# Gate sums in small steps, and the last row of each chunk one block ahead, in a fused recurrence and feed-forward kernel

## The chip, the cores and the metric

The kernel runs on one core of one Trainium2 chip. The metric is the device time of one execution in microseconds (us); of several executions the median counts. A core has TensorE (PE in the rows; the loading of its weights is PEld), VectorE (DVE), ScalarE (ACT), GpSimd (POOL), and SyncE (SP), which here issues every DMA. Each engine works through its own list of instructions in the order in which the program was built.

## What is computed

First a gated recurrence (mLSTM) over 768 steps for 4 batches with 8 heads of dimension 40, then a two-layer feed-forward network (320 to 2048 to 320) over the 3072 resulting rows:

```python
for t in range(S):
    m_new = np.maximum(f_gate[:, :, t] + m, i_gate[:, :, t])
    f_stab = np.exp(f_gate[:, :, t] + m - m_new)
    i_stab = np.exp(i_gate[:, :, t] - m_new)
    m = m_new
    C = f_stab[...] * C + i_stab[...] * np.einsum('bhd,bhe->bhde', vt, kt)
    n = f_stab[...] * n + i_stab[...] * kt
    h_tilde = np.einsum('bhde,bhe->bhd', C, qt)
    denom = np.maximum(np.abs(np.einsum('bhd,bhd->bh', n, qt)), 1.0)
    y[:, :, t] = sigmoid(o_gate[:, :, t]) * h_tilde / denom
h = y @ w_in
g = where(h >= 1, h, where(h <= -1, 0, (h + 1)**2 / 4))
out = g @ w_out
```

(The gates are abridged with "..." for added axes, and the sigmoid is written by name.)

## The kernel before

The 768 steps are cut into 6 chunks of 128, so that there are 24 pieces (chunk, batch), called rows here and numbered n = 4 * chunk + batch. The recurrence is done by chunk: inside a chunk it is a masked product of scores, and between chunks a state `C` is carried. The feed-forward network works on tiles of 512 tokens; tile j is chunk j of all four batches, so that rows 4j to 4j+3 make tile j, and tile j can begin only when its last row, 4j+3, is in `xh` and `xl` (y transposed and split in two words).

**The blocks.** Tile j has 16 blocks. Block x = 16 j + fc is `mm1` (8 products of 512 columns into a bank `psh`), the activation (`r`, on ACT twice and DVE once), the split of `r` into `gh` and `gl` (ACT, DVE), and two blocks later `mm2` (12 products of 320 columns into `pso`; 4 in tile 0). The loop over x at the end of the kernel sets the order in which all is written; a scheduler may then change the order within each engine's list.

**A row.** In the block that `OFFS` gives, a row of the next tile goes through `prep` (POOL masks the decay sums `Abc`, ACT takes 8 exponentials of them, POOL scales v), `score` (scores on PE, multiplied into `Abc` by DVE: the decayed scores), and `main` (PE: `psa<-C,qn` and then decayed scores times v; DVE: `hv`, `z`, `y`; PE: transposes `psa<-ident,y`; ACT: `CAST xh`; DVE: `xl`). `prep` stands 4 blocks ahead of `score`, `main` 3 blocks behind it, in three steps.

**Split scores.** From row 8 on, the decayed scores and v are cut into three bf16 parts (`parts3`: two instructions on DVE, `m<-Abc` and `v<-v`, and two on POOL for each row), and every head is multiplied in 6 part products: 48 products of 41 columns for a row. Rows 0 to 7 use the fp32 words: 8 products, which the trace shows as 16.

**Buffers.** `Abc` has three buffers. The DMA for row n+3 (`load_A`, from DRAM tensor `a_d`) is written in the first step of `main` of row n, and it waits until PE has read the scores of row n. It is issued by SP, like all others, in order.

**Gates.** For each chunk a piece of 16 small DVE instructions on 32 partitions (three of them scans), 3 on ACT, one on POOL, a transpose (`psa<-ident,ex`), the exponentials `G`, and 5 small DMAs (`a_d`, `dc_d`, three `dec`) gives the decays. Chunk j+2 is done in one go in block 3 of tile j, that is at x = 3, 19, 35 and 51.

Of the kernel before, what the change touches and what calls it, by code (L numbers as in the profile page):

```python
# [17 lines left out]
B, H, S, D = 4, 8, 768, 40  # L18
# [20 lines left out]

FRONT = 22  # L40
EARLY = 8
OFFS = [3, 5, 7, 9, 14, 18, 22, 25, 30, 34, 37, 40, 46, 48, 52, 56, 60, 66, 70, 74]
LEAD = 4
MLAG = 3
NA = 3
ST = 0

GFC = 3
DUE = lambda fc: 3 + fc


# [10 lines left out]
SPLIT_FROM = 8  # L62
# [33 lines left out]
def mlstm_ffn_kernel(ctx, tc, qk, qn, vk, og, fi0, fi, w_in, w_out, cst, out):  # L96
# [16 lines left out]
    later = ctx.enter_context(tc.tile_pool(name="later", bufs=1))  # L113
# [64 lines left out]
    exs = {}  # L178
    gtail = {}

    def gate_piece(c):
        gate_sums(c)
        gate_tail(c)
        gate_exps(c)

    def gate_sums(c):
        pool, i, f = gsrc.pop(c)

        NP = NSEQ if c else 3 * NSEQ
        new = lambda name, p=NP, n=L, bufs=1: pool.tile([p, n], F32, name=name if c else name + "0", bufs=bufs)  # L190
        k = 1
        m, a, ah, ac = new("m", n=L + 1, bufs=k), f, new("ah", bufs=k), new("ac")
        al = ah

        ex = exs[c] = new("ex", P)
        if c:
            nc.vector.tensor_copy(m[:, 0:1], carry)
        else:
            nc.vector.memset(m[:, 0:1], -1e30)
        nc.vector.tensor_tensor_scan(out=m[:, 1:], data0=f, data1=i, initial=m[:, 0:1], op0=ALU.add, op1=ALU.max)  # L200
        nc.vector.tensor_tensor(out=a, in0=f, in1=m[:, :L], op=ALU.add)
        nc.vector.tensor_tensor(out=a, in0=a, in1=m[:, 1:], op=ALU.subtract)

        nc.vector.tensor_scalar(out=ah, in0=a, scalar1=CLAMP, scalar2=GRID, op0=ALU.max, op1=ALU.add)
        nc.vector.tensor_scalar(out=ah, in0=ah, scalar1=-GRID, scalar2=None, op0=ALU.add)
        nc.vector.tensor_tensor_scan(out=ac, data0=rst[:NP], data1=ah, initial=0.0, op0=ALU.mult, op1=ALU.add)
        if c > 0:
            nc.sync.dma_start(a_d[c], ac)
            nc.scalar.copy(ex[64:96], ac)
        else:  # L210

            for p in (2 * NSEQ, NSEQ):
                nc.vector.tensor_tensor(out=ac[:p], in0=ac[:p], in1=top(ac[:p]), op=ALU.subtract)
            T["ac"] = ac
            m, a, ah, ac, al, i = (x[2 * NSEQ:] for x in (m, a, ah, ac, al, i))
            nc.gpsimd.tensor_copy(ex[64:96], ac)
        nc.vector.scalar_tensor_tensor(out=a, in0=a, scalar=CLAMP, in1=ah, op0=ALU.max, op1=ALU.subtract)
        reset = rst[:NSEQ] if c else rst[2 * NSEQ:]
        nc.vector.tensor_tensor_scan(out=al, data0=reset, data1=a, initial=0.0, op0=ALU.mult, op1=ALU.add)
        if c:  # L220
            nc.scalar.mul(ex[96:128], al, -1.0)
        else:
            nc.gpsimd.tensor_scalar(out=ex[96:128], in0=al, scalar1=-1.0, scalar2=None, op0=ALU.mult)
        nc.vector.tensor_copy(carry, m[:, L:])
        gtail[c] = i, m, a, ac, al, ex

    def gate_tail(c):
        i, m, a, ac, al, ex = gtail.pop(c)
        dh = m[:, :L]
        eng = nc.vector  # L230
        eng.tensor_tensor(out=a, in0=i, in1=m[:, 1:], op=ALU.subtract)
        eng.tensor_tensor(out=a, in0=a, in1=al, op=ALU.subtract)
        nc.gpsimd.tensor_copy(ex[0:32], a)
        eng.tensor_tensor(out=dh, in0=ac[:, L - 1:].broadcast_to([NSEQ, L]), in1=ac, op=ALU.subtract)
        eng.tensor_tensor(out=dh, in0=dh, in1=a, op=ALU.add)
        eng.tensor_tensor(out=ex[32:64], in0=dh, in1=al[:, L - 1:].broadcast_to([NSEQ, L]), op=ALU.add)
        eng.tensor_tensor(out=dc[:, c:c + 1], in0=ac[:, L - 1:], in1=al[:, L - 1:], op=ALU.add)

# [316 lines left out]
    def main(n):  # L555

        c, b = divmod(n, B)
        t = T.pop(n) if n >= B else T[n]
        g = gates_of(n)
        sg = sig[c][:, b, :]  # L560
        M = t["A"]
        if c > 0:
            C = state[b]
            ip = psum_a()
            for gi, h0 in enumerate(GROUPS):
                o = 6 - h0 if gi == 2 else 0
                nc.tensor.matmul(ip[:, (h0 + o) * D1:(h0 + 3) * D1], t["qn"][:, gi, :], C[:, gi, o * D1:3 * D1],
                                 start=True, stop=True)
            hv = wk.tile([P, H, D1], F32, name="hv", bufs=2)
            iv = ip[:, :H * D1].rearrange("p (h d) -> p h d", d=D1)  # L570
            nc.vector.tensor_tensor(out=hv, in0=iv, in1=g[:, 2, :].unsqueeze(2).broadcast_to([P, H, D1]), op=ALU.mult)
        up = psum_a()
        hot(up)
        if n < SPLIT_FROM:
            for h in range(H):
                nc.tensor.matmul(up[:, h * D1:(h + 1) * D1], M[:, h, :], t["v1"][:, h, :], start=True, stop=True)
        else:
            prod = [(i, k) for i in range(3) for k in range(3 - i)]
# [12 lines left out]
        if n >= B:
            load_A(n + NA)
        yield

        z = wk.tile([P, H], F32, name="z")
        nc.vector.scalar_tensor_tensor(out=z, in0=hv[:, :, D], scalar=-1.0, in1=g[:, 3, :], op0=ALU.mult, op1=ALU.max)
        nc.vector.tensor_tensor(out=z, in0=z, in1=hv[:, :, D], op=ALU.max)
        nc.vector.reciprocal(out=z, in_=z)
        sz = wk.tile([P, H, D], F32, name="sz", bufs=1)
        nc.vector.tensor_tensor(out=sz, in0=sg.rearrange("p (h d) -> p h d", d=D),  # L600
                                                     in1=z.unsqueeze(2).broadcast_to([P, H, D]), op=ALU.mult)
        y = wk.tile([P, DM], F32, name="y", bufs=2)
        nc.vector.tensor_tensor(out=y.rearrange("p (h d) -> p h d", d=D), in0=hv[:, :, 0:D], in1=sz, op=ALU.mult)
        if 0 < c < NC - 1:
            carry_on(n, t)
        yield

        xp = psum_a()
        hot(xp)
        for k in range(2):  # L610
            nc.tensor.transpose(xp[:, k * P:(k + 1) * P], y[:, k * P:(k + 1) * P], ident)
        nc.tensor.transpose(xp[:, 2 * P:3 * P], y[:, DM - P:], ident)
        if c == 0:
            yield
        j, r = divmod(n, NTC)
        if r == 0:
            X[j] = (xs.tile([P, 3, TT], F32R, name="xh"), xs.tile([P, 2, TT], F32R, name="xl"))
        xh, xl = X[j]
        cs = slice(r * L, (r + 1) * L)
        xv = xp[:, :3 * P].rearrange("p (k t) -> p k t", t=L)  # L620
        mark["x", "act"] = nc.scalar.copy(xh[:, :, cs], xv)
        mark["x", "dve"] = nc.vector.tensor_tensor(out=xl[:, :, cs], in0=xv[:, 0:2, :],
                                                   in1=xh[:, 0:2, cs].bitcast(F32), op=ALU.subtract)
        nc.vector.tensor_tensor(out=xh[0:64, 2, cs], in0=xv[64:128, 2, :], in1=xh[64:128, 2, cs].bitcast(F32),
                                op=ALU.subtract)
        yield
# [3 lines left out]
    for n in range(NS):  # L630
        j, r = divmod(n, NTC)
# [86 lines left out]
    for what in STEPS.split():  # L718
        n = int(what[1]) if what[1:2].isdigit() else 0
# [19 lines left out]
        elif what[0] == "m":  # L739
            score_mul(n, hh)  # L740
        elif what[0] == "g":
            gate_sums(n)
        elif what[0] == "k":
            gate_tail(n)
        elif what[0] == "h":
            gate_exps(n)
        elif what[0] == "A":
# [42 lines left out]
    for x in range(NG + LAG):  # L790
        j, fc = divmod(x, NFC)
        if x < NG:
# [8 lines left out]
            if j == 1 and fc % 2 == 0 and fc < PLAIN_FC:  # L801
                with tc.issue_after(mark["r", "act"].ins), tc.issue_after(mark["r", "dve"].ins):
                    for _ in split_out(fc // 2):
                        pass
            if j < 4 and fc == GFC:
                load_gates(later, j + 2, j + 3)
                with tc.issue_after(mark["r", "dve"].ins):
                    gate_piece(j + 2)
            r = mm1(j, fc)
            if x == 0:  # L810
                with tc.issue_after(mark["r", "dve"].ins):
                    gate_tail(1)
                    gate_exps(1)
            with behind(("v", "pool")):
                slot(FRONT + x)
# [62 lines left out]
```

## Time and profile before

| What | Value |
|---|---|
| Median of 3 executions | 531.85 us (530.48 to 534.66) |
| The profiled execution | 535.73 us, of it span 533.9 us |
| PE busy | 497.4 us, 93% |
| DVE busy | 366.4 us, 69% |
| ACT busy | 290.8 us, 54% |
| POOL busy | 146.4 us, 27% |
| Mean granted TensorE clock | 0.968 of full speed |
| Chain that ended last | PE 69%, DVE 12%, ACT 8%, DMA 6%, issue 2% |

The span is the time from the first to the last instruction. The granted clock is the share of full speed (2.4 GHz) that TensorE was given; 0.5 is its lower level. The idle time in brackets behind a row is what the engine waited before it, with the instruction that ended the wait.

### The profile page before, as it was taken

The page shows a single profiled execution, that of the slowest core. Times are in us where ns is not written, and L with a number is a line of the kernel's source. Part 1 is how long each engine was busy: PE and PEld are TensorE (multiplying, and loading weights), DVE is VectorE, ACT ScalarE, POOL GpSimd, SP SyncE. Part 2 cuts the span into 40 slices and gives each one's busy share as a digit, 9 for nine tenths or more (in the row PEclk, how much of TensorE's full clock was granted, in tenths as well). Part 3 has the DMA queues.
Part 4 walks back from the last instruction along what each step waited for, and adds up shares of the span by engine and source line. Part 5 has one row for each costly group of instructions (what it writes and reads, how often), then busy time and mean ns, then how long its engine had stood idle before and what let it go on. Part 6 is the DMA issues. An engine that isn't in the chain of part 4 may idle for free.

```text
span 533.9 us, 9184 instructions
## 1 busy us (share of the span) xinstructions
PE 497.4 (93%) x3527; PEld 421.8 (79%) x3527; DVE 366.4 (69%) x677; ACT 290.8 (54%) x576; POOL 146.4 (27%) x148
## 2 busy tenths in 40 slices
PE   7985989989899999989999979799999999999996
PEld 4753766768679889879888958598898898989886
DVE  4589988489759777769576848777757756444342
ACT  4525766544458664567644435754468344445553
POOL 2316522234333134343052515152411212000000
PEclk8987999979899999999999979999999999999999
DMA  7858555264342223252122234022333100010001
GB/s 218 243 162 264 182 150 170 83 207 153 85 154 68 48 61 104 79 155 76 30 78 72 84 103 152 3 83 100 111 106 114 40 0 1 2 49 2 1 1 50
DMA packets 29648, 51.31 MB, mean 96 GB/s; under 512 B 10124, under 2 KB 20004, under 8 KB 29604
## 3 DMA queue, kind: packets, MB, share of 16 engines
q1 hardware_dynamic: 29604, 50.72, 31.4%
q8 instruction: 28, 0.46, 0.3%
q14 instruction: 16, 0.13, 0.1%
HBM read 46.67 MB, written 4.04 MB: 95 GB/s over the span
## 4 chain that ended last, share of the span: by engine, by line
PE 69%; DVE 12%; ACT 8%; DMA 6%; issue 2%; POOL 1%; SPq 1%; ACTq 0%; DVEq 0%; POOLq 0%
PE psh L79 29%; PE pso L79 26%; PE psa L79 12%; ACT Abc L79 3%; DMA Abc<-a_d 2%; ACT r L79 2%; DMA wraw<-in_w_out 2%; PE pso L82 1%; DVE win L79 1%; DMA raw<-in_qk 1%; DVE r L79 1%; PE psa L82 1%; DVE mg L79 1%; POOL Abc L79 1%; DVE ow L79 1%
## 5 line engine op out<-in xcount | busy, mean ns | idle before, releaser
L79 ACT ACTIVATE r<-psh,half 128x512 f32<-128x512 f32 x96 | 65.3, 685 | 102.4 <-PE psh L79 101.1
L79 PE MATMUL psh<-xh,wh 128*128 128x512 f32 x288 | 105.6, 422 | 13.4 <-DVE r L79 12.0
L79 DVE SCALAR_TENSOR_TENSOR r<-psh,r 128x512 f32<-128x512 f32 x96 | 66.0, 687 | 65.2 <-ACT r L79 64.9
L79 PE MATMUL psh<-xh,wl 128*128 128x512 f32 x288 | 100.4, 404 | 0.0
L79 PE MATMUL pso<-oh,gh 128*128 128x320 f32 x320 | 99.4, 313 | 0.6 <-ACT gh L79 0.6
L79 PE MATMUL pso<-ow,gh 128*128 128x320 f32 x320 | 98.6, 310 | 0.0
L79 PE MATMUL pso<-oh,gl 128*128 128x320 f32 x320 | 91.1, 310 | 0.0
L79 DVE TENSOR_TENSOR gl<-r,gh 128x512 fp32r<-128x512 f32 x80 | 61.0, 765 | 28.3 <-ACT gh L79 27.7
L79 ACT CAST gh<-r 128x512 fp32r<-128x512 f32 x80 | 49.5, 618 | 51.2 <-DVE r L79 49.9
L79 PEld LDWEIGHTS psh<-xh,wh 128*128 128x128 f32 x288 | 51.8, 195 | 24.1 <-DVE r L79 14.5
L79 PEld LDWEIGHTS psh<-xh,wl 128*128 128x128 f32 x288 | 55.8, 195 | 13.1 <-DVE m L82 0.4
L79 ACT ACTIVATE Abc<-Abc,nA 128x128 f32<-128x128 f32 x160 | 49.6, 390 | 29.7 <-POOL Abc L79 29.7
L79 PEld LDWEIGHTS pso<-oh,gh 128*128 128x128 f32 x320 | 60.1, 188 | 4.5 <-ACT gh L79 0.8
L79 PE MATMUL psh<-xl,wh 128*128 128x512 f32 x192 | 62.5, 408 | 0.0
L79 PEld LDWEIGHTS pso<-ow,gh 128*128 128x128 f32 x320 | 60.1, 188 | 2.8
L79 ACT ACTIVATE r<-r 128x512 f32<-128x512 f32 x96 | 60.3, 632 | 2.2
L79 PEld LDWEIGHTS pso<-oh,gl 128*128 128x128 f32 x320 | 58.0, 188 | 0.3
L79 POOL TENSOR_TENSOR v<-vk,G 128x328 f32<-128x328 f32 x36 | 31.5, 879 | 53.6 <-issue 29.8
L79 POOL TENSOR_TENSOR m<-m 128x1024 bf16<-128x1024 f32 x16 | 31.2, 1953 | 51.8 <-DVE m L79 40.6
L79 PEld LDWEIGHTS psh<-xl,wh 128*128 128x128 f32 x192 | 37.0, 195 | 8.5
L79 PE MATMUL pso<-ow,r 128*128 128x320 f32 x128 | 39.9, 457 | 0.5 <-DVE ow L79 0.5
L79 POOL TENSOR_TENSOR C<-C,dec 120x369 f32<-120x369 f32 x16 | 13.8, 859 | 91.7 <-PE psa L79 91.7
(187 smaller groups left out, 742.0 us busy)
## 6 DMA issues: line engine op xcount, KB each, us to landing
Abc<-a_d SPq DMA_DIRECT2D x20, 512.0 KB
raw<-in_qk SPq DMA_DIRECT2D x48, 160.0 KB
vk<-in_vk SPq DMA_DIRECT2D x20, 324.0 KB
wraw<-in_w_in SPq DMA_DIRECT2D x8, 768.0 KB
wraw<-in_w_out SPq DMA_DIRECT2D x8, 640.0 KB
sig<-in_og SPq DMA_DIRECT2D x6, 640.0 KB
out<-r SPq DMA_DIRECT2D x24, 160.0 KB
qn<-in_qn SPq DMA_DIRECT2D x20, 180.0 KB
```

The source lines that it names most:

```text
L79: r = getattr(self.engine, name)(*args, **kwargs)
L82: r = getattr(self.engine, name)(*args, **kwargs)
```

## The change

Three edits. First, the gate pieces of chunks 2 to 5 are generators that are taken one step per block. They begin at x = 2, 13, 28 and 43 instead of being done at once at x = 3, 19, 35 and 51; each has eight steps with instructions (scan; two adds; two roundings; scan, `a_d` and the first copy; second scan; three steps of the tail), and a ninth that is empty. Second, in `OFFS` five entries are one less: row 10, and rows 11, 15, 19 and 23, the last rows of chunks 2 to 5. Third, for these four last rows the decayed scores are not cut into parts.

```diff
-OFFS = [3, 5, 7, 9, 14, 18, 22, 25, 30, 34, 37, 40, 46, 48, 52, 56, 60, 66, 70, 74]
+OFFS = [3, 5, 7, 9, 14, 18, 21, 24, 30, 34, 37, 39, 46, 48, 52, 55, 60, 66, 70, 73]
-GFC = 3
+GATES_AT = (2, 13, 28, 43)
...
-    def gate_piece(c):
-        gate_sums(c)
-        gate_tail(c)
+    def gate_steps(c):
+
+        yield from gate_sums(c)
+        yield from gate_tail(c)
         gate_exps(c)
+        yield
...
-        if n < SPLIT_FROM:
+        if n < SPLIT_FROM or b == B - 1:
...
-            if j < 4 and fc == GFC:
-                load_gates(later, j + 2, j + 3)
+            if x in GATES_AT:
+                c = 2 + GATES_AT.index(x)
+                load_gates(later, c, c + 1)
+                steps = gate_steps(c)
+            if x >= GATES_AT[0]:
                 with tc.issue_after(mark["r", "dve"].ins):
-                    gate_piece(j + 2)
+                    next(steps, None)
```

Inside `gate_sums` and `gate_tail` the only edits are the added `yield` lines.

How the lists of the engines change, at three places. (Line numbers: most instructions go through one helper, line 79 before and 80 in the change.)

**ACT at the start of tile 3.** Abc_3187 before, and Abc_3059 in the change, is the buffer of row 18, whose DMA waits for row 15; the second `CAST xh` is that of row 15. Before:

```order
L79 CAST xh_2650<-psa_3082 128x3x128
L79 ACTIVATE r_3367<-r_3367 128x512
L79 CAST gh_3374<-r_3367 128x512
L79 ACTIVATE Abc_3187<-Abc_3187,nA_122 128x128 x6
L79 CAST xh_2650<-psa_3282 128x3x128
L79 ACTIVATE Abc_3187<-Abc_3187,nA_122 128x128 x2
L79 ACTIVATE r_3403<-psh_3394,half_118 128x512
```

And in the change:

```order
L80 CAST xh_2604<-psa_3036 128x3x128
L80 CAST gh_3265<-r_3241 128x512
L80 ACTIVATE r_3294<-psh_3285,half_118 128x512
L80 ACTIVATE r_3294<-r_3294 128x512
L80 ACTIVATE ex_3091<-ah_3089 32x128
L80 CAST gh_3301<-r_3294 128x512
L80 ACTIVATE Abc_3059<-Abc_3059,nA_122 128x128 x8
L80 CAST xh_2604<-psa_3158 128x3x128
L80 ACTIVATE r_3333<-psh_3324,half_118 128x512
```

All eight exponentials of row 18 stand ahead of the `CAST xh` of row 15, where six did. At the start of tile 2 the eight of row 14 stand ahead of the `CAST xh` of row 11 in both.

**PE at the start of tile 2.** raw_1812 before, and raw_1716 in the change, holds q and k of row 12 for its scores; `ident,y` are the transposes of row 11, `C,qn` the first product of row 12's `main`. Before:

```order
L79 MATMUL psa_2299<-raw_1812 128x128
L79 MATMUL psa_2300<-raw_1812 128x128
L79 MATMUL psa_2313<-ident_98,y_2257 128x128 x3
L79 MATMUL psa_2431<-C_1540,qn_1879 128x123 x2
L79 MATMUL psa_2431<-C_1540,qn_1879 128x82
L79 MATMUL psh_2383<-xh_1623,wh_131 128x512 x2
L79 MATMUL psh_2383<-xh_1623,wl_132 128x512 x2
```

And in the change:

```order
L80 MATMUL psa_2231<-ident_98,y_2184 128x128 x3
L80 MATMUL psa_2272<-raw_1716 128x128
L80 MATMUL psh_2356<-xh_1615,wh_131 128x512 x2
L80 MATMUL psh_2356<-xh_1615,wl_132 128x512 x2
L80 MATMUL psh_2394<-xh_1615,wh_131 128x512 x2
L80 MATMUL psh_2394<-xh_1615,wl_132 128x512 x2
L80 MATMUL psh_2356<-xl_1616,wh_131 128x512 x2
L80 MATMUL psh_2394<-xl_1616,wh_131 128x512 x2
L80 MATMUL psa_2273<-raw_1716 128x128
```

Before, all eight `raw` products and the `C,qn` products stand ahead of the first `mm1` of tile 2; in the change one `raw` product does, and the rest come behind it. In both lists the score product of row 11 has the whole of block 31 of `mm1` ahead of it and 24 `mm2` products behind it before the first `mm1` of tile 2. At the start of tile 3 the score product of row 15 has 12 `mm2` products behind it before that point in the list before, and 22 in the change.

**DVE in tile 3.** m_3610, fi_t_3608, ah_3611 and ac_3612 before, and m_3088, fi_t_3086, ah_3089 and ac_3090 in the change, belong to the gate piece of chunk 5. Before, from a block's `r` on:

```order
L79 SCALAR_TENSOR_TENSOR r_3566<-psh_3557,r_3566 128x512
L79 COPY m_3610<-carry_126 32x1
L79 SCALAR_TENSOR_TENSOR m_3610<-fi_t_3608,m_3610 32x128
L79 TENSOR_TENSOR fi_t_3608<-fi_t_3608,m_3610 32x128
L79 COPY carry_126<-m_3610 32x1
L79 TENSOR_TENSOR hv_3464<-psa_3466,hv_3464 128x328
L79 TENSOR_TENSOR gl_3594<-r_3566,gh_3592 128x512
L79 TENSOR_TENSOR m3_3676<-Abc_3003 128x1024
```

And in the change, from the same block's `gl` on:

```order
L80 TENSOR_TENSOR m_3088<-m_3088,fi_t_3086 32x128
L80 TENSOR_TENSOR gl_3360<-r_3333,gh_3358 128x512
L80 TENSOR_TENSOR hv_3396<-psa_3392,G_121 128x328
L80 TENSOR_TENSOR ex_3091<-m_3088,ah_3089 32x128
L80 TENSOR_TENSOR gl_3463<-r_3385,gh_3461 128x512
L80 TENSOR_TENSOR hv_3396<-psa_3398,hv_3396 128x328
L80 TENSOR_TENSOR m3_3584<-Abc_2960 128x1024
L80 SCALAR_TENSOR_TENSOR r_3510<-psh_3501,r_3510 128x512
```

Of the 16 instructions of the piece four are left behind the start of tile 3; before, all 16 stand there.

On SP, in tile 0, `dc_d` and `dec` of chunk 2 stood directly ahead of a load `wraw<-in_w_out` of weights; in the change that load and four further loads of weights precede them.

## Rows read from the trace of the kernel before

**Rows 1.** The page: busy time, share of the span and count of each engine, and PE's busy tenths in 40 slices of the span.

```profile
PE 497.4 (93%) x3527; PEld 421.8 (79%) x3527; DVE 366.4 (69%) x677; ACT 290.8 (54%) x576; POOL 146.4 (27%) x148
...
PE   7985989989899999989999979799999999999996
```

**Rows 2.** Busy time by stage: the stage, its length, then busy us (and count) of PE, PEld, DVE, ACT and POOL, the granted clock, the DMA share and GB/s.

```profile
60.00:70.00 10.00, 8.70 (x42) 6.63 (x41) 9.42 (x18) 9.93 (x31) 4.79 (x6) 1.00 0.30 84
...
330.00:340.00 10.00, 7.72 (x42) 6.66 (x41) 9.66 (x22) 4.15 (x9) 4.25 (x4) 1.00 0.02 5
...
235.00:300.00 65.00, 64.41 (x512) 57.22 (x512) 48.26 (x88) 40.16 (x80) 20.39 (x18) 1.00 0.24 70
...
311.00:318.00 7.00, 6.78 (x30) 5.01 (x29) 1.24 (x3) 1.04 (x4) 0.00 (x0) 0.65 0.12 43
```

**Rows 3.** The chain that ended last, in order of time (start, us, what): one `mm1` and one `mm2` of the steady state.

```profile
247.02 1.86 PE psh L79 x8
248.88 1.75 PE pso L79 x12
```

**Rows 4.** The start of tile 3 (block 48), in order of time by engine: start, us, engine, what, count, and idle time before it with what ended it. The first PE row follows the score product of row 15, 309.67 are its transposes, 311.49 is the first `mm1` of block 48, 321.23 that of block 50; the DMA, the mask and the exponentials of `Abc` are those of row 18.

```profile
303.95 0.87 PE L79 MATMUL psa<-v,vk 128*120 128x123 f32 x6
...
309.67 0.87 PE L79 MATMUL psa<-ident,y 128*128 128x128 f32 x3 [3.09 <-DVE y L79]
...
311.49 1.22 PE L79 MATMUL psh<-xh,wh 128*128 128x512 f32 x2 [0.22 <-ACT xh L79]
...
321.23 0.72 PE L79 MATMUL psh<-xh,wh 128*128 128x512 f32 x2 [1.26 <-DVE r L79]
...
304.06 0.33 SPq L79 DMA_DIRECT2D Abc<-a_d  x1
...
308.09 1.09 POOL L79 TENSOR_SCALAR_AFFINE_SELECT Abc<-Abc 128x1024 f32<-128x1024 f32 x1 [0.29 <-DMA Abc<-a_d]
...
309.22 1.86 ACT L79 ACTIVATE Abc<-Abc,nA 128x128 f32<-128x128 f32 x6 [4.92 <-POOL Abc L79]
310.98 0.46 ACT L79 CAST xh<-psa 128x384 fp32r<-128x384 f32 x1
```

**Rows 5.** The start of tile 2 (block 32), in the same columns. 221.60 is the first of row 11's score products, 222.84 follows the last of them, 231.47 is the first `mm1` of block 32, 238.89 that of block 34; the DMA, the mask and the exponentials are those of row 14.

```profile
221.60 0.25 PE L79 MATMUL psa<-v,Abc 128*128 128x41 bf16 x3 [0.51 <-DVE hv L79]
...
222.84 0.88 PE L79 MATMUL psa<-v,vk 128*120 128x123 f32 x6
...
231.47 0.73 PE L79 MATMUL psh<-xh,wh 128*128 128x512 f32 x2 [0.40 <-ACT xh L79]
...
238.89 0.50 PE L79 MATMUL psh<-xh,wh 128*128 128x512 f32 x1
...
222.95 0.33 SPq L79 DMA_DIRECT2D Abc<-a_d  x1
...
227.23 1.34 POOL L79 TENSOR_SCALAR_AFFINE_SELECT Abc<-Abc 128x1024 f32<-128x1024 f32 x1
...
228.61 2.45 ACT L79 ACTIVATE Abc<-Abc,nA 128x128 f32<-128x128 f32 x8 [4.18 <-POOL Abc L79]
```

**Rows 6.** An uncut score product (row 6) and the instruction behind it, the first of the 48 part products of row 15, which end where the first of rows 4 begins; and from the groups of instructions (count, busy us, mean ns) the cut of the scores on DVE.

```profile
125.42 1.92 PE L79 MATMUL psa<-v,Abc 128*128 128x41 f32 x16
127.17 0.87 PE L79 MATMUL psa<-v,vk 128*120 128x123 f32 x6
...
302.71 0.24 PE L79 MATMUL psa<-v,Abc 128*128 128x41 bf16 x3
...
L79 DVE TENSOR_TENSOR m<-Abc 128x1024 f32<-128x1024 f32 x16 | 20.1, 1257 | 0.2
```

**Rows 7.** The gate piece of chunk 5 in tile 3: on DVE the first and the tenth of its 16 instructions and the `r` behind them, and the waits of PE that follow.

```profile
327.50 0.13 DVE L79 COPY m<-carry 32x1 f32<-32x1 f32 x1
...
337.00 0.41 DVE L79 TENSOR_TENSOR_SCAN ah<-rst,fi_t 32x128 f32<-32x128 f32 x1
337.34 0.65 DVE L79 SCALAR_TENSOR_TENSOR r<-psh,r 128x512 f32<-128x512 f32 x1
...
338.04 0.73 PE L79 MATMUL psh<-xh,wh 128*128 128x512 f32 x2 [2.27 <-DVE r L79]
...
341.19 0.42 PE L79 MATMUL pso<-oh,gh 128*128 128x320 f32 x1 [0.59 <-ACT gh L79]
...
344.17 0.73 PE L79 MATMUL psh<-xh,wh 128*128 128x512 f32 x2 [0.94 <-DVE r L79]
```

**Rows 8.** Tile 0: the first and the last DVE instruction of the gate piece of chunk 2 (16 in all), the wait of PE behind it, and the load of weights that SP issued behind the piece's DMAs.

```profile
53.59 0.13 DVE L79 COPY m<-carry 32x1 f32<-32x1 f32 x1
...
65.51 0.28 DVE L79 TENSOR_TENSOR ex<-m,ah 32x128 f32<-32x128 f32 x1
...
70.84 1.58 PE L79 MATMUL psa<-raw 40*128 40x128 f32 x16 [2.13 <-DVE C L79]
...
69.48 0.39 SPq L79 DMA_DIRECT2D wraw<-in_w_out  x1
```

**Rows 9.** A wait of PE for DVE late in tile 0, and DVE's own idle time at the starts of tiles 2 and 3.

```profile
138.35 1.95 PE L79 MATMUL psa<-v,Abc 128*128 128x41 f32 x16 [1.32 <-DVE xh L79]
...
237.25 0.50 DVE L79 TENSOR_TENSOR hv<-psa,hv 128x328 f32<-128x328 f32 x1 [4.12 <-PE psa L79]
...
317.48 1.29 DVE L79 TENSOR_TENSOR Abc<-psa,Abc 128x512 f32<-128x512 f32 x2 [5.25 <-PE psa L79]
```

More of the change, by code (lines that the diff above doesn't have):

```diff
@@ L179, in mlstm_ffn_kernel, with run @@
     gtail = {}
-    def gate_piece(c):
-        gate_sums(c)
-        gate_tail(c)
+    def gate_steps(c):
+        yield from gate_sums(c)
+        yield from gate_tail(c)
         gate_exps(c)
+        yield
+    def run(steps):
+        for _ in steps:
+            pass
     def gate_sums(c):
@@ L200, in gate_sums @@
         nc.vector.tensor_tensor_scan(out=m[:, 1:], data0=f, data1=i, initial=m[:, 0:1], op0=ALU.add, op1=ALU.max)
+        yield
         nc.vector.tensor_tensor(out=a, in0=f, in1=m[:, :L], op=ALU.add)
         nc.vector.tensor_tensor(out=a, in0=a, in1=m[:, 1:], op=ALU.subtract)
+        yield
         nc.vector.tensor_scalar(out=ah, in0=a, scalar1=CLAMP, scalar2=GRID, op0=ALU.max, op1=ALU.add)
         nc.vector.tensor_scalar(out=ah, in0=ah, scalar1=-GRID, scalar2=None, op0=ALU.add)
+        yield
         nc.vector.tensor_tensor_scan(out=ac, data0=rst[:NP], data1=ah, initial=0.0, op0=ALU.mult, op1=ALU.add)
@@ L209, in gate_sums @@
             nc.scalar.copy(ex[64:96], ac)
+            yield
         else:
@@ L225, in gate_sums @@
         gtail[c] = i, m, a, ac, al, ex
+        yield
     def gate_tail(c):
@@ L233, in gate_tail @@
         nc.gpsimd.tensor_copy(ex[0:32], a)
+        yield
         eng.tensor_tensor(out=dh, in0=ac[:, L - 1:].broadcast_to([NSEQ, L]), in1=ac, op=ALU.subtract)
         eng.tensor_tensor(out=dh, in0=dh, in1=a, op=ALU.add)
+        yield
         eng.tensor_tensor(out=ex[32:64], in0=dh, in1=al[:, L - 1:].broadcast_to([NSEQ, L]), op=ALU.add)
@@ L741, in mlstm_ffn_kernel @@
         elif what[0] == "g":
-            gate_sums(n)
+            run(gate_sums(n))
         elif what[0] == "k":
-            gate_tail(n)
+            run(gate_tail(n))
         elif what[0] == "h":
@@ L811, in mlstm_ffn_kernel @@
                 with tc.issue_after(mark["r", "dve"].ins):
-                    gate_tail(1)
+                    run(gate_tail(1))
                     gate_exps(1)
```

## The prediction

> **What bounds the kernel now.** Read the page's totals first [rows 1]: PE is busy 93% of the span, and in the 40 slices its dips stand in few places. The stages [rows 2] say which: from 235 to 300 us PE is busy 64.4 of 65 us, so nothing that other engines save there is worth anything; at 60 to 70 and at 330 to 340 us DVE is busy 9.4 and 9.7 of 10 us, and PE loses 1.3 and 2.3. The steady block costs 1.86 + 1.75 = 3.61 us of PE [rows 3]. So time is PE's work plus PE's idle time plus what a lowered clock adds. The timeline around the starts of tiles then shows the larger losses [rows 4, 5].
>
> At the start of tile 3 [rows 4] PE waits 3.09 us for `y` of row 15, then 0.22 for its `CAST xh`, and at 311 to 318 us the granted clock is 0.65 [rows 2], that is mostly 1.2 GHz. Follow `Abc` beside it: when PE has read row 15's scores (303.95), SP issues the load of row 18 (304.06), POOL masks it (308.09), ACT starts its exponentials (309.22), and the `CAST xh` of row 15 stands behind six of them (310.98), although row 18 is not due until tile 3. At the start of tile 2 [rows 5] the same chain runs from 222.84 to the first `mm1` at 231.47, 8.63 us, but there PE had other work and idled little.
>
> All sums are against the profiled execution, 535.73 us (span 533.9 and 1.83 around it). It is 3.9 us above the median of 531.85; I put the sum of differences on the median.
>
> **The change part by part.**
>
> *Uncut scores.* An uncut row takes 127.17 - 125.42 = 1.75 us of PE, a cut one 303.95 - 302.71 = 1.24 [rows 6, 4]: +0.51 for each of four rows. Rows 19 and 23 lie where PE is full, so +1.0; those of rows 11 and 15 are counted in the two tile starts below. What it takes from DVE (1.26 us for the scores of each row [rows 6]) and from POOL lies beside full PE, as from 235 to 300 us [rows 2]: nothing. The Trainium skill, "TensorE: Matmul & The Clock Gate", section "Back-to-back issue gap", gives products of 1 to 64 columns some 25 ns each whatever their width. By it the 16 instructions of an uncut row would be an estimated 0.4 us, and each row would save 0.8 instead of costing 0.5, the sum below coming out some 5 us lower; the row, which is this very operation, shows 109 ns apiece, so this gets no chance.
>
> *Start of tile 2: +3.4.* The list of ACT still has row 14's eight exponentials ahead of row 11's `CAST xh`, and as much `mm1` and `mm2` lies around row 11's product as before. So the product ends where it did (+0.51 for the uncut scores, -0.51 for the wait for `hv` [rows 5], now covered by earlier `C,qn`), and `mm1` of block 32 again follows 8.6 us later. But `raw` and `C,qn`, which filled that time, now come behind it, and PE stands idle longer. That is how tile 3 starts already, also with its `raw` products between the `mm1`; there block 50 follows block 48 by 321.23 - 311.49 = 9.74 us [rows 4], here block 34 follows block 32 by 7.42 [rows 5]: +2.3. By that time 43 of row 12's 48 part products, done before, are still open: 43/48 x 1.24 = +1.1. Least: the 1.1 alone; most: another 3 if the clock stays low as long again. I take 3.4, since the new list is that of rows 4.
>
> *Start of tile 3: -0.3.* Ten `mm2` products move from ahead of row 15's product to behind it: 10 x 1.75/12 = -1.5 [rows 3], +0.5 for the uncut scores. From there the chain through row 18 decides as before, and all eight exponentials are ahead of the cast where six were: two more of 2.45/8 [rows 5], +0.6. Together -0.3. So the wait for `y` goes and the wait for ACT takes its place, with the low clock. Ends: +0.7 (the 8.63 us of rows 5 instead of the 7.54 of rows 4) and -7 (first rival).
>
> *Gates of chunk 5: -3.3.* At 327.5 to 337.4 us ten of its instructions stand ahead of a block's `r`, which PE then awaits 2.27 us; 0.59 and 0.94 follow [rows 7]. The ten are 3.2 us by their rows; four short ones, 1.0 us, now stand in front instead. So `r` is 2.2 us earlier; with the 0.59 and half of the 0.94 that makes 3.3. Ends: 0, if another instruction is late in its place, and all 3.8. The steps that go to blocks 43 to 47 are covered by full PE. The pieces of chunks 3 and 4 left blocks 19 and 35, where PE did not wait [rows 2]: 0 for their removal.
>
> *Gates of chunk 2: -2.0.* The 16 instructions between 53.6 and 65.8 us [rows 8] sit in the fullest stretch of DVE; behind them PE waits 2.13 us for DVE at 70.84. Spread to later blocks, and with `dc_d` and `dec` no longer ahead of the load at 69.48, nearly all of that should go. Ends: 0 and -2.1.
>
> *Gates of chunk 3: +1.2.* Their first steps go to blocks 13 to 16, at the end of tile 0, where PE does wait for DVE, 1.32 us at 138.35 [rows 9]. Seven instructions of the kind of rows 7 are some 2.4 us; I take half as seen. Ends: 0 and +2.4.
>
> Sum: 1.0 + 3.4 - 0.3 - 3.3 - 2.0 + 1.2 = 0.0, hence 531.9 us. The change removes waits and puts as many in their place.
>
> **The rivals.**
>
> *The last row's step works* (faster). If `CAST xh` is not held by the next row's exponentials, because the load lands sooner or the row ends so much earlier that the chain is over in time, then at tile 3 the 3.09 + 0.22 + 1.26 us [rows 4] go and so does the low clock (7.0 us at 0.65 [rows 2] is 2.4 us), 7.0 in all, and tile 2 costs the least, 1.1. That is -6.7 and -2.3 against the sum: 522.9, and half of it 527. For it: `y` stood in front in rows 4, not ACT. Against it: the order of ACT's list is fixed, and the chain of 7.5 to 8.6 us was there both times.
>
> *Steps over the tile starts* (slower). Chunks 3, 4 and 5 now have their steps over blocks 16, 32 and 48, where DVE serves stores, scores, `y` and `r` at once. If half of a piece of 4.7 us (16 instructions, at the durations of those of rows 7) is seen by PE at each, that is 3 x 2.35 = 7 us: 539. It decides from where DVE's idle time before the work of a tile is used up; that was 4.12 and 5.25 us [rows 9], which speaks against it, but `r` must come through this queue before PE can go on.
>
> *The change doesn't do what it says.* The lists show the last row's product still behind the last `mm1` of its tile. If then tile 2 also goes as before (0 instead of 3.4, with 0.5 for its uncut row), only gates and uncut scores are left: 0.0 - 3.4 + 0.5 = -2.9: 529.
>
> **How the numbers follow.** A measurement of this kernel can tell about 1%, 5.3 us, from no change. Chances: forecast 0.42, the last row's step 0.23, steps over the tile starts 0.20, no effect of the step 0.15. The first and the last lie within 1% except for 0.05 of the forecast's on the fast side and 0.02 on the slow; the half form of the fast rival (0.03) stays within. So faster 0.25, same 0.53, slower 0.22. The range of 524 to 539.5 takes in the slow rival and most of the fast one; the forecast's own, with its terms' ends partly offsetting, is 527 to 536.
>
> **What would show it.** Right: in the changed profile PE idles 3 to 4 us before the first `mm1` of tile 2 with ACT's `CAST xh` directly behind eight `Abc` exponentials, and a granted clock near 0.65 behind it; the same at tile 3, with `ACT xh` rather than `DVE y` as what ended the wait; no wait above 1 us for `r` in tile 3 from 330 us on; PE's wait near 70 us gone; uncut products at 1.75 us. Wrong: if the tile starts run without a wait (first rival), or if PE waits for `r` of blocks 18, 34 and 50 longer than 2 us with gate instructions ahead of it on DVE (second).

## The result, and the profile after

| | Before | After |
|---|---|---|
| Median of 20 executions each | 533.16 us (530.42 to 539.43) | 537.5 us (531.58 to 542.47) |
| Ratio of the times | | 1.0058, 95% interval 1.003 to 1.0085 |
| The profiled execution | 535.73 us | 538.07 us |

The ratio, here and below, compares the runs in the faster of two states in which executions come, and the medians are of all runs. The change is 0.3 to 0.85% slower, about 3 us, and so within the 1% that the prediction called no change. Read the totals and the slices of the changed kernel first.

```profile
PE 501.1 (93%) x3396; PEld 427.1 (80%) x3399; DVE 359.7 (67%) x669; ACT 291.5 (54%) x576; POOL 138.8 (26%) x140
...
PE   8957999798997999969999979999999999999996
PEclk9987999899797999988999988999999999999999
```

PE has fewer instructions than in [rows 1], since an uncut row shows 16 products where a cut one has 48, for four rows, but it is busy 3.7 us longer, and the granted clock is 0.958 on average instead of 0.968. The stages after the change say where (stage, length, busy us and count of PE, PEld, DVE, ACT and POOL, granted clock, DMA share, GB/s):

```profile
165.00:175.00 10.00, 10.00 (x43) 8.82 (x43) 7.00 (x16) 6.39 (x12) 0.00 (x0) 0.71 0.10 6
232.00:246.00 14.00, 12.82 (x57) 9.86 (x57) 8.38 (x16) 6.78 (x11) 4.21 (x3) 0.76 0.29 92
317.00:325.00 8.00, 7.30 (x39) 5.55 (x41) 2.57 (x6) 1.64 (x4) 0.00 (x0) 0.79 0.26 84
```

The first two windows of the kernel before, in the same columns:

```profile
165.00:175.00 10.00, 10.00 (x57) 9.02 (x57) 9.62 (x26) 8.03 (x19) 3.03 (x3) 1.00 0.12 36
232.00:246.00 14.00, 13.41 (x120) 11.48 (x119) 9.28 (x20) 10.74 (x19) 6.19 (x6) 1.00 0.44 132
```

A full-looking window hides the loss: in the first, PE is busy 10 of 10 us in both kernels, but at 0.71 of full speed, that is partly at 1.2 instead of 2.4 GHz.

To compare kernels whose starts differ, I cut each trace at the instruction `r` of DVE (96 of them, one for each block). In a stage, idle time is its length less PE's busy time, and the clock's share is its length times (1 - granted clock), from the two digits that a view prints, so that it is good to some 0.3 us. The profiled execution of before reaches block 0 at 47.04 us, all thirteen others between 41.8 and 43.4; that part of its 535.73 us belongs to that execution, so everything counts from block 0. Idle / clock in us (e1 to e10 are the experiments below):

| Blocks | before | after | e1 | e2 | e3 | e9 | e10 |
|---|---|---|---|---|---|---|---|
| 0-16 | 9.4 / 8.4 | 8.4 / 9.3 | 8.8 / 10.3 | 9.2 / 8.4 | 7.5 / 9.2 | 9.5 / 8.4 | 8.2 / 9.7 |
| 16-24 | 0.1 / 0 | 3.4 / 3.6 | 3.4 / 1.8 | 0.1 / 0 | 0.4 / 0 | 0.1 / 0 | 3.5 / 1.5 |
| 24-40 | 2.2 / 0 | 4.3 / 3.6 | 4.5 / 1.9 | 5.2 / 5.1 | 2.3 / 0 | 4.5 / 3.2 | 1.1 / 1.9 |
| 40-56 | 8.8 / 3.2 | 4.5 / 3.4 | 2.6 / 0 | 7.1 / 3.1 | 5.7 / 3.2 | 9.1 / 4.9 | 2.4 / 0 |
| 56-95 | 0.4 / 0 | 0 / 0 | 0 / 0 | 3.3 / 2.9 | 0 / 0 | 0.4 / 0 | 1.4 / 0 |
| Length | 478.6 | 485.1 | 478.1 | 492.4 | 473.0 | 485.5 | 475.2 |

After against before: idle time in all -0.4, clock +8.2, length +6.5. (The parts do not add up to the length: PE's work differs too, and the clock's share also counts a low clock while PE idles.) These are single executions, and the two differ by more than the 3 us that the ratio gives: read from the stages where time went, and from the ratios how much. The waits of PE moved, and the new ones stand where a lowered clock follows them. By place, the change is 0.8 us shorter up to block 16, 6.2 longer from block 16 to 28, 5.2 longer from 28 to 40, 0.6 shorter from 40 to 48 and 3.5 shorter behind that.

**The start of tile 2**, in order of time (start, us, engine, what, idle before); it answers to [rows 5]:

```profile
221.67 1.87 PE L80 MATMUL psa<-v,Abc 128*128 128x41 f32 x16
223.38 0.87 PE L80 MATMUL psa<-v,vk 128*120 128x123 f32 x6
...
229.92 0.52 PE L80 MATMUL psa<-ident,y 128*128 128x128 f32 x3 [2.17 <-DVE y L80]
...
231.80 0.88 PE L80 MATMUL psh<-xh,wh 128*128 128x512 f32 x2 [0.94 <-ACT xh L80]
...
228.94 2.45 ACT L80 ACTIVATE Abc<-Abc,nA 128x128 f32<-128x128 f32 x8 [4.52 <-POOL Abc L80]
231.29 0.45 ACT L80 CAST xh<-psa 128x384 fp32r<-128x384 f32 x1
```

PE idles 2.17 + 0.94 us, where before it had `raw` and `C,qn` to do. At the start of tile 3, [rows 4], the sum of the two waits is nearly the same as before, 3.25 against 3.31 us:

```profile
307.67 1.88 PE L80 MATMUL psa<-v,Abc 128*128 128x41 f32 x16
309.37 0.88 PE L80 MATMUL psa<-v,vk 128*120 128x123 f32 x6
...
315.83 0.52 PE L80 MATMUL psa<-ident,y 128*128 128x128 f32 x3 [2.31 <-DVE y L80]
...
317.70 1.22 PE L80 MATMUL psh<-xh,wh 128*128 128x512 f32 x2 [0.94 <-ACT xh L80]
...
326.91 0.72 PE L80 MATMUL psh<-xh,wh 128*128 128x512 f32 x2 [1.26 <-DVE r L80]
...
310.92 0.49 DVE L80 TENSOR_TENSOR hv<-psa,hv 128x328 f32<-128x328 f32 x1
...
315.19 0.49 DVE L80 TENSOR_TENSOR y<-hv,sz 128x320 f32<-128x320 f32 x1
...
314.85 2.44 ACT L80 ACTIVATE Abc<-Abc,nA 128x128 f32<-128x128 f32 x8 [4.59 <-POOL Abc L80]
317.20 0.46 ACT L80 CAST xh<-psa 128x384 fp32r<-128x384 f32 x1
```

PE's transposes end at 316.35, but the `CAST xh` begins at 317.20, when row 18's exponentials are through: of the two waits that of ACT ends last, and the first `mm1` follows it.

**The start of tile 1** has a wait that was not there before, 3.30 us for the `r` of block 18:

```profile
164.81 1.22 PE L80 MATMUL psh<-xh,wh 128*128 128x512 f32 x2 [3.30 <-DVE r L80]
...
155.73 4.72 POOL L80 TENSOR_SCALAR_AFFINE_SELECT Abc<-Abc 128x1024 f32<-128x1024 f32 x1 [3.17 <-DMA Abc<-a_d]
...
160.48 0.99 ACT L80 ACTIVATE Abc<-Abc,nA 128x128 f32<-128x128 f32 x3 [2.16 <-POOL Abc L80]
161.38 0.67 ACT L80 ACTIVATE r<-psh,half 128x512 f32<-128x512 f32 x1
...
163.41 0.62 ACT L80 ACTIVATE r<-r 128x512 f32<-128x512 f32 x1
...
159.42 1.17 DVE L80 TENSOR_TENSOR fi_t<-fi_t,ah 32x128 f32<-32x128 f32 x1
...
164.06 0.69 DVE L80 SCALAR_TENSOR_TENSOR r<-psh,r 128x512 f32<-128x512 f32 x1 [2.53 <-ACT r L80]
```

Follow it back: DVE waits for ACT's `r`, which stands behind three exponentials of row 11's `Abc`, which wait for POOL's mask; and the mask took 4.72 us where it takes 1.09 and 1.34 in [rows 4, 5]. Before, the first activation of block 18 stood ahead of those exponentials in ACT's list, and the second ahead of the other five; in the change they stand behind three and behind all eight. In the kernel before:

```profile
161.71 0.69 ACT L79 ACTIVATE r<-psh,half 128x512 f32<-128x512 f32 x1
...
163.71 0.99 ACT L79 ACTIVATE Abc<-Abc,nA 128x128 f32<-128x128 f32 x3
164.61 0.62 ACT L79 ACTIVATE r<-r 128x512 f32<-128x512 f32 x1
```

The order is that of e1 too, so it comes with the steps and not with the new places.

### The profile page after: what moved, and what is told of

It is laid out like the page before. It is cut to its first block, busy times and chain, and to the rows that moved or that the text cites. A ratio compares the mean times of both kernels' runs of the same rounds, so it can differ in the third digit from the quotient of the medians.

```text
span 536.3 us, 8899 instructions
## 1 busy us (share of the span) xinstructions
PE 501.1 (93%) x3396; PEld 427.1 (80%) x3399; DVE 359.7 (67%) x669; ACT 291.5 (54%) x576; POOL 138.8 (26%) x140
## 4 chain that ended last, share of the span: by engine, by line
PE 75%; DVE 7%; ACT 7%; issue 3%; POOL 3%; DMA 3%; SPq 0%; ACTq 0%; POOLq 0%; DVEq 0%
PE psh L80 31%; PE pso L80 27%; PE psa L80 13%; ACT Abc L80 3%; POOL Abc L80 2%; PE psa L83 2%; DMA Abc<-a_d 2%; ACT r L80 1%; PE pso L83 1%; POOL v L80 1%; DVE r L80 1%; PE psh L83 1%; DVE win L80 1%; DVE ow L80 1%; DMA wraw<-in_w_out 1%
## 5 line engine op out<-in xcount | busy, mean ns | idle before, releaser
L80 PE MATMUL psh<-xh,wh 128*128 128x512 f32 x288 | 107.4, 429 | 14.8 <-DVE r L80 12.2
L80 PE MATMUL psh<-xh,wl 128*128 128x512 f32 x288 | 103.6, 414 | 0.0
L80 PE MATMUL pso<-oh,gl 128*128 128x320 f32 x320 | 93.3, 313 | 0.0
L80 PEld LDWEIGHTS psh<-xh,wh 128*128 128x128 f32 x288 | 53.1, 199 | 24.9 <-DVE r L80 13.9
L80 POOL TENSOR_TENSOR v<-vk,G 128x328 f32<-128x328 f32 x36 | 29.7, 829 | 67.2 <-issue 43.7
L80 POOL TENSOR_TENSOR C<-C,dec 120x369 f32<-120x369 f32 x16 | 13.7, 856 | 111.0 <-PE psa L80 111.0
L80 DVE TENSOR_TENSOR Abc<-psa,Abc 128x512 f32<-128x512 f32 x40 | 25.9, 680 | 17.8 <-PE psa L80 17.8
```

The costliest lines, as they stand in the source:

```text
L80: r = getattr(self.engine, name)(*args, **kwargs)
```

## The experiments

Ratios are to the kernel before, run beside them on the same chip, with 95% intervals.

| | Kernel | Median us | Ratio |
|---|---|---|---|
| e1 | gates in steps alone | 529.27 | 0.9918 (0.9887 to 0.995) |
| e2 | new places and uncut scores alone | 544.11 | 1.0167 (1.0112 to 1.0223) |
| e3 | steps for chunks 2 and 5 alone | 525.36 | 0.9851 (0.982 to 0.9883) |
| e4 | the change, row 11's exponentials behind block 18 | 535.42 | 1.0043 (1.0013 to 1.0073) |
| e5 | new places alone | 546.05 | 1.0242 (1.0197 to 1.0287) |
| e6 | uncut scores alone | 531.1 | 0.996 (0.9928 to 0.9991) |
| e7 | the change, idle time filled | 533.07 | 0.9998 (0.9966 to 1.0031) |
| e8 | e3, idle time of tile 3 filled | 525.87 | 0.9871 (0.9821 to 0.992) |
| e9 | new place of row 11 alone | 540.16 | 1.0149 (1.0124 to 1.0175) |
| e10 | the change, rows 12 and 16 earlier too | 526.23 | 0.9889 (0.9864 to 0.9913) |
| e11 | e3, row 16 earlier | 524.92 | 0.986 (0.9833 to 0.9887) |
| e12 | e11, uncut scores | 526.81 | 0.9909 (0.9878 to 0.994) |

**e1 and e2: the change in two halves.** e1 is the change with the old `OFFS` and the old condition for the cut; e2 is the kernel before with

```diff
-OFFS = [3, 5, 7, 9, 14, 18, 22, 25, 30, 34, 37, 40, 46, 48, 52, 56, 60, 66, 70, 74]
+OFFS = [3, 5, 7, 9, 14, 18, 21, 24, 30, 34, 37, 39, 46, 48, 52, 55, 60, 66, 70, 73]
-        if n < SPLIT_FROM:
+        if n < SPLIT_FROM or b == B - 1:
```

> The kernel before with the gates in steps alone (old places of the last rows, scores cut as before). Theory 1, the steps of chunk 3 over the start of tile 1 are what costs, through ACT's list, in which the first activation of block 18 now stands behind three exponentials of Abc: about 535 to 537 us against 533.2, with PE waiting more than 2 us for r in blocks 18 to 20 and then a lowered clock, and the waits of tile 3 gone. Theory 2, as forecast, the lists that the uncut scores and the earlier last rows open at the starts of tiles 2 and 3 are what costs, and steps only give: 533.2 - 3.3 - 2.0 + 1.2, about 529 us, and no such wait.

> The kernel before with the other two parts alone: the last rows one block ahead and uncut, gates at one go in blocks 3, 19, 35 and 51. Theory 1: no wait above 1 us in blocks 16 to 20, and within 2 us of the kernel before. Theory 2: 533.2 + 1.0 + 3.4 - 0.3, about 537 us, with 3 us of idle PE and a low clock at the start of tile 2.

The halves have opposite signs, as theory 2 says: the steps gain 0.8%, 4.4 us, the other half costs 1.7%, 8.9 us, and together they make 0.85% where the change has 0.58. e1's time is the forecast's, 529. e2 misses it by far: its terms made 4.1 us, and it lost 8.9. In its trace 7.9 of 13.7 us lie behind block 56 (idle time 3.3, clock 2.9 in the table), and in that of e5 below 8.9 of 14.5; the change has nothing there. So the new places cost more with the gates done at one go than in the change (why was not isolated), and that the halves nearly add up is in part chance. Yet theory 1's wait is in e1 as well, and a second one of its kind at the start of tile 2, behind a slow mask:

```profile
166.45 0.80 PE L80 MATMUL psh<-xh,wh 128*128 128x512 f32 x1 [3.30 <-DVE r L80]
...
250.59 0.73 PE L80 MATMUL psh<-xh,wh 128*128 128x512 f32 x2 [2.52 <-DVE r L80]
...
242.14 4.10 POOL L80 TENSOR_SCALAR_AFFINE_SELECT Abc<-Abc 128x1024 f32<-128x1024 f32 x1 [3.09 <-ACT r L80]
```

So the steps gain although they pay for these.

**e3: what the steps of chunks 3 and 4 cost.**

```diff
-GATES_AT = (2, 13, 28, 43)
+GATES_AT = {2: 2, 19: 3, 35: 4, 43: 5}
...
-                    next(steps, None)
+                    for _ in range(9 if c in (3, 4) else 1):
+                        next(steps, None)
```

(on e1; chunks 3 and 4 take all steps at once, as before).

> The kernel before with the steps for chunks 2 and 5 alone (from blocks 2 and 43); chunks 3 and 4 at one go in blocks 19 and 35, last rows as before. Both theories: 2.0 and 3.3 us less than before, about 528 us, faster by 1%. If it is 533, the two gains of the forecast are not there.

It gained 1.5%, 7.9 us of 533.2, more than expected, and neither wait of e1 is there. The steps of chunks 3 and 4 therefore cost 529.27 - 525.36 = 3.9 us; at blocks 19 and 35 their pieces cost PE next to nothing (0.4 us of idle time in blocks 16 to 24, and as much as before in 24 to 40).

**e4: is it ACT's order?**

```diff
+            with behind(*[("r2", 18)] * (n == 11)):
-            nc.scalar.activation(A[:, h, :], src, AF.Exp, bias=bias)
+                nc.scalar.activation(A[:, h, :], src, AF.Exp, bias=bias)
```

(`r2` marks the second activation of a block.)

> The changed kernel with one order added: ACT's exponentials of row 11 stand behind both activations of block 18 and no longer ahead of them. Theory 1: the wait of 3.3 us for r at the start of tile 1 goes and the lowered clock behind it too, 537.5 becomes 532 to 534. Rival: the slow mask of POOL and the gate steps on DVE hold r anyway, and the time stays at 537.

Start of tile 1 in e4 (POOL's mask and ACT's list):

```profile
155.33 1.09 POOL L80 TENSOR_SCALAR_AFFINE_SELECT Abc<-Abc 128x1024 f32<-128x1024 f32 x1 [2.72 <-DMA Abc<-a_d]
...
157.10 0.69 ACT L80 ACTIVATE r<-psh,half 128x512 f32<-128x512 f32 x1
157.82 0.63 ACT L80 ACTIVATE r<-r 128x512 f32<-128x512 f32 x1
...
159.77 2.46 ACT L80 ACTIVATE Abc<-Abc,nA 128x128 f32<-128x128 f32 x8
```

The wait is gone, and the lowered clock behind it (1.00 from 160 to 175 us); blocks 16 to 24 are 3.6 us shorter than in the change. But the mask is fast here too, after a load that landed 0.4 us earlier, so the run does not part order from mask. And the ratios of e4 and the change, 1.0043 and 1.0058, overlap: that the whole gained is not shown, only that the stage did.

**e5, e6 and e9: which of the places and uncut scores costs.** e5 has the diff of `OFFS` above alone, e6 that of the condition alone, e9 the kernel before with one entry less:

```diff
-OFFS = [3, 5, 7, 9, 14, 18, 22, 25, 30, 34, 37, 40, 46, 48, 52, 56, 60, 66, 70, 74]
+OFFS = [3, 5, 7, 9, 14, 18, 22, 24, 30, 34, 37, 40, 46, 48, 52, 56, 60, 66, 70, 74]
```

> The kernel before with the last rows' new places alone. Theory: the loss of 9 us of the two parts together comes from the places, since with them the raw and C,qn products of row 12 stand behind the first mm1 of tile 2: 4 us or more of idle PE there with a lowered clock behind it, about 539 to 541 against 533.2. Rival: it is the uncut scores, and this one stays at 533 to 535.

> The kernel before with the uncut scores of rows 11, 15, 19 and 23 alone; the list of PE at the start of tile 2 stays as it was (raw and C,qn ahead of the first mm1). Theory: four times 0.5 us and no new wait, 534 to 535.5. Rival: the uncut scores are what costs, 538 or more.

> The kernel before with row 11 alone one block earlier (24 instead of 25). Since score(12) comes at x = 30 and the transposes of row 11 now at x = 29, the raw products of row 12 take their banks psa behind the transposes. Theory: this one entry is most of the loss of the places, PE idles 3 us or more before the first mm1 of tile 2 and the clock takes 3.4 us behind it, 533.2 + 5 to 8, about 539 to 541. By the forecast's term for the start of tile 2 it is 533.2 + 2.9, 536. Rival: the loss is spread over all the places, and this one stays within 2 us.

The places cost 2.4%, more than both parts together (the intervals of e5 and e2 overlap); the uncut scores gain 0.4%, just clear of nothing, where four times 0.5 us were to be lost. In e9 the one entry for row 11 costs 1.5%, 7.9 us of 531.92:

```profile
218.48 0.87 PE L79 MATMUL psa<-v,vk 128*120 128x123 f32 x6
...
224.70 0.52 PE L79 MATMUL psa<-ident,y 128*128 128x128 f32 x3 [1.85 <-DVE y L79]
...
226.52 1.22 PE L79 MATMUL psh<-xh,wh 128*128 128x512 f32 x2 [0.89 <-ACT xh L79]
...
234.72 0.22 PE L79 MATMUL psa<-v,m 128*128 128x41 bf16 x2 [0.88 <-DVE m L79]
...
235.73 0.73 PE L79 MATMUL psh<-xh,wh 128*128 128x512 f32 x2
```

The clock is low at the start (0.57 from 226 to 230 us), and once more behind block 34's first `mm1`:

```profile
236.00:240.00 4.00, 4.00 (x12) 3.13 (x12) 2.15 (x4) 3.96 (x7) 1.18 (x1) 0.57 0.42 150
```

From block 28 to 40 its trace is 5.2 us longer than before, as is that of the change: the loss of the change at tile 2 is that of this entry.

The code says why: `psa` has two banks, given out in the order of writing. With row 11 at 25 its transposes are written at x = 30, in the slot in which row 12's two score banks are taken first; at 24 they are written at x = 29, take a bank ahead of them, and 7 of 8 `raw` products must wait until that bank has been read. Before, the start of tile 3 already had this order (transposes of row 15 at x = 45, scores of row 16 at 46), which is why [rows 4] show the idle time and [rows 5] don't.

e6 shows the hold on ACT that the prediction spoke of, at the start of tile 3:

```profile
306.79 1.22 PE L79 MATMUL psh<-xh,wh 128*128 128x512 f32 x2 [2.86 <-ACT xh L79]
...
303.93 2.44 ACT L79 ACTIVATE Abc<-Abc,nA 128x128 f32<-128x128 f32 x8 [5.63 <-POOL Abc L79]
306.28 0.46 ACT L79 CAST xh<-psa 128x384 fp32r<-128x384 f32 x1
```

**e7 and e8: does the idle time bring the low clock?** Into the bank that `mm1` then overwrites (10 in tiles 2 and 3 of the change; 12 in tile 3 of e3; `up` marks the `psa<-v,vk` products behind the row's scores):

```diff
+        for _ in range({2: 10, 3: 10}.get(j, 0) if fc == 0 else 0):
+            with behind("up"):
+                nc.tensor.matmul(hp, wh[:, 0, 0:P], wh[:, 1, 0:TT], start=True, stop=True)
```

> The changed kernel with ten products of 512 columns, 2.2 us in all, behind the products of rows 11 and 15, into the bank of block 32 and 48 which mm1 then overwrites; they fill PE's wait for y. Theory: the low clock behind the starts of tiles 2 and 3 comes from the idle time there, so idle time is replaced by filling at no cost and the 3.4 us that the clock takes at each shrink to 1.7 or nothing: 537.5 becomes 531 to 535. Rival: the clock is low there for another reason, and the time stays at 537.5 or grows by up to 2.

> The kernel with the steps for chunks 2 and 5 alone, and twelve such products, 2.6 us, behind the product of row 15, in the 3.1 us in which PE waits for y at the start of tile 3. Theory: the lowered clock behind that start (3.4 us lost from 302 to 312 us) goes, 525.4 becomes 522 to 523.5. Rival: 525.4 or more.

In e7 PE no longer waits for `y` at tile 2:

```profile
222.53 2.55 PE L80 MATMUL psh<-wh 128*128 128x512 f32 x10
...
228.44 0.49 PE L80 MATMUL psa<-ident,y 128*128 128x128 f32 x3
```

The first `mm1` comes no earlier (230.29 - 221.90 = 8.39 us behind row 11's product, 8.42 in the change). From block 24 to 56 the clock takes 1.7 us instead of 7.0, and useless work made the kernel about 0.6% faster, the two intervals just touching: the low clock there follows from the idle time, at least in part. (The clock of one trace is no fine measure: behind the wait of 3.3 us at the start of tile 1 it takes 3.6 us in the change and 1.5 to 1.8 in e1, e7 and e10.) In e8 it halved too (1.6 instead of 3.2 us between blocks 40 and 48), but the 3.0 us of products took the place of 2.75 us of waiting and the wait for `CAST xh` grew from 0.22 to 1.47; no gain.

**e10: the loss undone.**

```diff
-OFFS = [3, 5, 7, 9, 14, 18, 21, 24, 30, 34, 37, 39, 46, 48, 52, 55, 60, 66, 70, 73]
+OFFS = [3, 5, 7, 9, 14, 18, 21, 24, 29, 34, 37, 39, 44, 48, 52, 55, 60, 66, 70, 73]
```

> The changed kernel with rows 12 and 16 earlier too (29 and 44 instead of 30 and 46), so that their scores are written ahead of the transposes of rows 11 and 15, and the raw products take their banks first. Theory: the idle time at the starts of tiles 2 and 3 and the low clock behind them go at least in part: 537.5 becomes 529 to 533. Rival: the wait for y and for ACT holds PE all the same, 536 or more.

It is 1.1% faster than before, some 9 us better than the change, by two numbers that put the scores' banks ahead of the transposes' again. The first `mm1` of tile 2 is not earlier (230.91 - 222.11 = 8.80 us behind row 11's product), but `raw` fills the time until `y`:

```profile
226.11 0.48 PE L80 MATMUL psa<-raw 40*128 40x128 f32 x2
...
226.87 1.16 PE L80 MATMUL psa<-raw 40*128 40x128 f32 x14
...
229.00 0.67 PE L80 MATMUL psa<-ident,y 128*128 128x128 f32 x3 [0.63 <-DVE Abc L80]
```

At tile 2 the clock still takes 1.9 us (table); at tile 3 the low clock is gone:

```profile
300.00:330.00 30.00, 27.60 (x211) 23.42 (x210) 21.52 (x45) 19.98 (x41) 11.10 (x11) 1.00 0.43 128
```

It is gone in e1 too, and the intervals of e10 and e1 overlap: the two numbers take the loss of the new places back, and that these places then gain anything is not shown.

**e11 and e12: a version that beats both.** e11 is e3 with row 16 at 45, e12 the same with the uncut condition.

> The kernel with the steps for chunks 2 and 5 alone, and row 16 one block earlier (45 instead of 46), so that half of its raw products fill PE's wait at the start of tile 3. Theory: up to 2 of the 3.1 us of that wait and half or all of the 3.4 us of low clock go, 525.4 becomes 521 to 523.5. Rival: as in the filled one, no gain, 525 to 526.

> The same, and the scores of rows 11, 15, 19 and 23 uncut. If the gain of the uncut scores alone (2 us) adds, 519 to 522; if it came only from the start of tile 3 and the late gates, which are already changed here, no different from the one before, or 1 to 2 us more for the longer products.

e11 equals e3 within its interval: PE still waits 2.54 us at tile 3, now for DVE's work on the scores that came earlier. In e12 the gain of e6 doesn't add; it is 2 us slower than e11, with intervals that overlap. e3 and e11, at 525 us, are the fastest.

## Why the prediction was right, and where it was wrong

*The outcome.* "No change" held, and 537.5 lies in the range; but the sum of 0.0 should have been some +3 us, and it came out near because gains and losses were both larger than thought: that the total was hit is partly luck. The stages of the change say it by place: the start of tile 1, for which the sum has no term and only the second rival a price, costs 6.2 us, the largest loss of all; tile 2 costs 5.2 instead of 3.4; tile 3 and what follows gain 4.1.

*Gates of chunks 2 and 5* (-2.0 and -3.3): right in place and mechanism, in sum somewhat small. The waits of 2.13 at 70.84 us and of 2.27, 0.59 and 0.94 in tile 3 [rows 7, 8] have no counterpart in the change. e3 gains 7.9 us by its ratio and 5.65 from block 0 on in its trace, of it 1.7 up to block 16 and 4.65 from block 48.

*Gates of chunk 3* (+1.2) and the 0 for chunk 4: mis-sized and misplaced. Together they cost 3.9 us (e3 against e1). I looked for the cost at the end of tile 0, on DVE; it came at the start of tile 1, 3.30 us of wait and 3.6 of clock, by way of ACT's list and POOL's mask. The order of ACT's list there was to be had before the run. (That blocks 19 and 35 were free before, [rows 2] show for block 35 alone; for block 19 the table does, with 0.1 us of idle time in blocks 16 to 24.)

*Start of tile 2* (+3.4): right cause, the term mis-sized. Without the 0.5 for the uncut row it was 2.9; e9 measures 7.9 by its ratio, and in its trace 5.2 between blocks 28 and 40. That block 34 follows block 32 by 9.74 instead of 7.42 us nearly held: in e9 it is 235.73 - 226.52 = 9.21, with 0.88 of waiting for row 12's cut in it. The step that failed is where the sum stops: behind these two blocks the clock fell a second time, to 0.57 from 236 to 240 us, which is 1.7 us. The prediction knew the price ("another 3 if the clock stays low") and left it to the range. The rest of e9's loss, 1.9 us between blocks 40 and 48 in its trace, lies at instructions that were reordered with it, as far as I can tell; I didn't separate it further. Of the signs named, the idle time of 3 to 4 us (3.1) and the eight exponentials ahead of `CAST xh` are there; the clock shows 0.76 over 14 us and not 0.65 over 7, the same loss in two pieces.

*Start of tile 3* (-0.3): right in what decides, wrong in where the wait shows. Idle time and clock are as before (3.25 against 3.31 us; 3.4 against 3.2). The chain through row 18 and ACT ends last, and the first `mm1` follows row 15's product by 317.70 - 309.37 = 8.33 us, where 7.54 + 0.6 was forecast. But the wait for `y` did not go: DVE takes 4.8 us from `hv` to the end of `y`, so that most of the idle time stands ahead of the transposes, and ACT's hold adds 0.94 to it. In e6, where `y` is early, ACT's hold is all of the wait (2.86).

*Uncut scores* (+0.5 each): the instruction is right, 223.38 - 221.67 = 1.71 us, 107 ns for each of 16. The floor of some 25 ns that the Trainium skill gives in "TensorE: Matmul & The Clock Gate", section "Back-to-back issue gap", is not what limits it. What failed, as far as e6 shows it, is "nothing" for what DVE and POOL save: e6 is 2 us faster instead of 2 slower, with PE idle 3.3 instead of 5.0 us between blocks 48 and 56 and 0.9 instead of 2.1 between 24 and 32. Which of the 1.26 us cuts gave that was not isolated, and in e12 there is no such gain.

*The rivals.* That the last row's step works is out for the change (both tile starts wait). e10, two numbers away, has tile 2 start without that wait, but not by this rival's mechanism: the chain there is as long as ever, and PE has other work beside it. That steps over the tile starts cost was half right: its sign, a wait above 2 us for the `r` of block 18, is there, at one start of three; but the gate instructions ahead of it on DVE were done by then and DVE idled 2.53 us for ACT, so the threshold that I gave, DVE's idle time, was the wrong one. That the change does nothing at tile 2 is refuted.

## What to carry to other kernels

Price a wait of PE together with the clock behind it, and follow that to where the clock is back, not to the next block: here three microseconds of idle time cost 1.5 to 3.6 more. When a step is moved, look at what it passes in the order in which buffers are given out; one block in the written order decided whether the filler for a wait could run in it. Split an edit of three parts before judging it: the part worth keeping gained 1.5%, and it was hidden by the steps of two chunks, which lost 0.7%, and by one number that alone lost 1.5%.

## What the hardware showed that I had not expected

The mask of POOL (`Abc<-Abc`, 128x1024) takes 1.1 to 1.7 us at the start of tile 1 in ten of the kernels, and 4.72, 4.78, 4.62 and 4.88 in the change, e1, e7 and e10, which have the same lists there. In the change it begins at 155.73 and ends at 160.45, while DVE works without a gap on seven instructions, six of which read two operands from SBUF; the gate step at 159.42 among them then took 1.17 us instead of its usual 0.27, and ended with the mask. e4 has the same list of DVE up to there, and the mask begins 0.4 us earlier, takes 1.09, and it is DVE's `gl` beside it that is longer. Two rows of the change, then that `gl` in e4:

```profile
156.07 0.80 DVE L80 TENSOR_TENSOR ow<-ow,oh 128x640 fp32r<-128x640 f32 x1
156.81 0.67 DVE L80 TENSOR_TENSOR gl<-r,gh 128x512 fp32r<-128x512 f32 x1
...
157.02 1.22 DVE L80 TENSOR_TENSOR gl<-r,gh 128x512 fp32r<-128x512 f32 x1
```

That the two engines kept each other out is read from these rows and not shown by a run that took DVE's instructions away. The Trainium skill, "SBUF — State Buffer", section "SBUF: two separate sides", has it that the two engines share a port pair, and that of a GpSimd instruction and a VectorE instruction with two SBUF inputs the one that starts first holds it for the whole instruction. The trace agrees with holding; but in the change the mask's row begins 0.34 us ahead of the first of those instructions, and yet POOL lost the pair for a row of them and not for one.

Ten useless products of 2.5 us in a wait made PE faster behind it (e7): what is saved lies between the two levels of the clock, 1.2 and 2.4 GHz, and the granted clock of a stage shows it, not its busy time.
